# Sliding-window attention and a highway layer on one core: q and k loaded two tokens of each 64 to a partition, the set-up cut in pieces, the bias of 12 blocks added by ScalarE, and a new written order

## The chip, the core and the metric

The kernel runs on one core of a Trainium2 chip. The metric is the device time of one execution in microseconds (us). The engines are TensorE (PE; its weight loads are listed as PEld), VectorE (DVE), ScalarE (ACT), GpSimd (POOL) and SyncE (SP), each with a queue of its own that is worked off in order. An engine waits for another only where its next instruction needs it. Transfers are issued from POOL's queue (loads, with a cast from float32 to bfloat16) and SP's queue (stores), and run on 16 DMA engines.

## The reference

There are 8 batches, 8 heads, 576 tokens and a head size of 64. Attention is causal with a window of 128 tokens and a linear bias by distance (ALiBi); its output, heads side by side, is the input x of a highway layer.

```python
scores = scale * np.matmul(q, k.transpose(0, 1, 3, 2))
bias = slopes[:, None, None] * (-np.abs(rel))[None, :, :]
mask = (rel >= 0) & (rel < window)
scores = np.where(mask, scores + bias[None], -1000000000.0)
attn = softmax(scores)
x = np.matmul(attn, v)          # [4608, 512] after putting heads side by side
H = np.maximum(x @ w_h, 0.0)
T = 1.0 / (1.0 + np.exp(-(x @ w_t + b_t)))
return T * H + (1.0 - T) * x
```

q, k, v, the weights and the result are float32; the kernel multiplies in bfloat16.

## The kernel before

The work is cut into 32 stages of scores, four for each batch, and 36 blocks of 128 rows of x: four for each batch, and one for every two batches that holds the last 64 rows of both. All steps are small functions (`load`, `tr`, `scores` and so on). The string `ORDER` names one step per letter, and the letters are worked off from left to right; each engine's queue is the order in which its instructions come up. `BANKS` gives the PSUM bank of each step in turn.

A batch goes through these steps. POOL issues five loads (L111, L117): q and k for each group of four heads, and v. A q or k load puts 18 consecutive tokens of a head into each of 128 partitions, 4608 bytes read in one piece; v is read in pieces of 256 bytes. DVE transposes q and k in 32x32 squares of 4-byte words (`tr`, L178), so that a pair of head elements lies in a partition and the tokens lie along it; the words of a square's row are written 18 words, 72 bytes, apart. Two buffers of each hold the loads (`LD`) and the transposed data (`TR`), so every second batch uses the same one. PE makes the scores (`scores`, L206 and, in the last stage of a batch, L216), 32 small matmuls to a stage, each on 32 rows of the array. In eight stages, listed in `ADD`, PE first writes the bias and the mask into PSUM with four matmuls on a table `MA` (L198); POOL has made that table (L168). ACT takes the exponential (`soft`, L233). In the 24 other stages DVE multiplies the result by a table `MK` or `MK3` that holds the exponential of the bias, or zero outside the window (`mask`, L240).

PE multiplies by v in two halves (`pv`, steps p and y, L273); a column of ones beside v gives the sum for the softmax. Before each second half stands a drain of PE. DVE divides (`norm`, L282 and L283), PE transposes the block (L292), ACT copies it to SBUF (L297), and PE multiplies by `wH` (L302) and by `wT` (L323). The bias b_t is added to the second product by one more matmul with a row of ones (L325). What follows is elementwise: relu by ACT (L312, then a subtraction of x by DVE, L317) or by DVE alone (L308); tanh by ACT (L329); a scaling to the gate by ACT (L334) or DVE (L336); the product with the gate by DVE or POOL (L342); the final addition by POOL or DVE (L347); and the store from SP (L353, L357). Capital letters in `ORDER` choose the other engine.

The set-up stands at the head of `ORDER`: `clear` (step R) fills all constant parts of the buffers on DVE, then four loads are issued, then `setup` (step S) makes the tables on POOL, DVE and ACT. The first v load comes after it in POOL's queue. A load waits until the load eight before it has landed, since eight semaphores are used in turn.

Of the kernel before, what the change touches and what calls it, by code (L numbers as in the profile page):

```python
# [9 lines left out]
P = 128  # L10
NB, NS, NG, NH = 8, 4, 2, 4
NP, NP3, NT = 5, 3, 18
ADD = ((0, 1), (1, 1), (2, 1), (3, 1), (4, 1), (5, 1), (6, 1), (7, 1))

ORDER = (
    "RLLLLSTLTLLTLLTLLLsseesmLesepmpLyynnpxymcxchLnLpUhvxLTycznLhauTxtzUGcTzaLvthToazUgLdDOsa"
    "gdvesOLDdgsmeLToesLTdeppymyLnpnyxLTcxchnhTxzcuLUmsaheLvTpzUmLyasvnpTexyznLcTsaxheDDgLpTy"
    "cosuhGednzDOxLUmsdczavmephLDTaGyUsntGpTexyLzOcOdsanhLdeLvzguoxTascdpmehLDmyznUtppgaxvyOy"
    "cpndhnxUygzcnoxTaxhdcvcLDsmtLheuhgUpTGsUTLyepnyLnxscOzeOdxvdhvamcsDuhGeTpzoTUypLdanzLtvL"
    "smaxyemznGtsaTcGxtzTeopTyoadschnedhgDOUxuGsdcTpehOyvzdnUsmaxzemvptTypapycnytznxnaxhcgtTG"  # L20
    "xUscTGcheTohuhdUOsOUdzevdvvzmastmapzegmyoznatdDpmaxycppnypygxnyochnxdnhcuxUxgpcDhOvydGUh"
    "nzvuoxasdzctehGzUoascvdtmhageDpozUygdsanzeOxvdptsmaycgztnoehGdxuzaocpthmdayUDzGnpvaxgyoc"
    "pnhodyUxnzcdvDxahgcozuDdhgaOzUDdgvOaDdgOd"
)
BANKS = (
    "0404024010210402101240404602323014021402340124012430242014012402346020140124012402430140"
    "2146076045605460467045602540124012401420140260452320612134201402140124012302340201401201"
# [3 lines left out]
def lists():  # L31

    stages = [(b, s) for b in range(NB) for s in range(NS)]
    blocks = []
    for b, s in stages:
        blocks.append((b, s))
        if s == NS - 1 and b % 2:
            blocks.append((b // 2, NS))
    loads = []
    for b in range(NB):  # L40
        loads += [(w, b, g) for g in range(NG) for w in "kq"]
        loads += [("v", b)]
        if b == 0:
            loads += [("w", 0), ("w", 1), ("w", 2)]
    by = dict(L=loads, T=[x for x in loads if x[0] in "kq"])
    by.update({k: stages for k in "se"})
    by["m"] = [x for x in stages if x not in ADD]
    by["v"] = []
    by.update({k: blocks for k in "pynxchuzatgod"})
    return by  # L50
# [3 lines left out]
def kernel(  # L54
# [26 lines left out]
    SQ = S + 64  # L81
# [9 lines left out]
    LD = {(i, g, w): cp.tile([P, NT * D], BF16, name=f"ld{i}{g}{w}")  # L91
          for i in range(2) for g in range(NG) for w in "qk"}
    TR = {(i, g, w): cp.tile([P, SQ, 2], BF16, name=f"tr{i}{g}{w}")
          for i in range(2) for g in range(NG) for w in "qk"}
# [9 lines left out]
    MA = cp.tile([P, NH, 2, 192], BF16, name="ma")  # L104
    MK3 = cp.tile([P, NH, 2, 256], BF16, name="mk3")
    PS = pp.tile([P, 8, 512], F32, name="ps")

    def load(kind, *at):
        if kind in "qk":
            b, g = at  # L110
            nc.gpsimd.dma_start(  # L111
                out=LD[b % 2, g, kind][:],
                in_=(q if kind == "q" else k)[b, 4 * g : 4 * g + 4].rearrange(
                    "h (s t) d -> (h s) (t d)", t=NT))
# [13 lines left out]
    def clear():  # L128
        for i in range(NB):
            nc.vector.memset(VA[i][:, :, D : D + 1], 1.0)  # L130
        nc.vector.memset(ones0[:], 0.0)
        nc.vector.memset(ones0[0:1, :], 1.0)
        nc.vector.memset(ident[:], 1.0)
        for p in PB:
            nc.vector.memset(p[:, :, 0:64], 0.0)
            nc.vector.memset(p[:, :, 256:320], 0.0)
            nc.vector.memset(p[:, :, 512:576], 0.0)
        for p in PE3:
            nc.vector.memset(p[:, :, 0:64], 0.0)
        for i in range(2):  # L140
            for g in range(NG):
                for w in "qk":
                    nc.vector.memset(TR[i, g, w][:, S:SQ, :], 0.0)
        nc.vector.memset(bT[:], 0.0)

    def setup():
        rel_i = cp.tile([P, 192], I32, name="rel_i")
        rel = cp.tile([P, 192], F32, name="rel")
        over = cp.tile([P, 192], F32, name="over")
        for half in range(2):  # L150
            nc.gpsimd.iota(rel_i[half * D : (half + 1) * D, :], pattern=[[1, 192]], base=0,
                           channel_multiplier=-1)
        nc.gpsimd.affine_select(
            out=ident[:], in_=ident[:], compare_op=ALU.is_equal, fill=0.0,
            base=0, pattern=[[1, P]], channel_multiplier=-1)
        nc.vector.tensor_copy(out=rel[:], in_=rel_i[:])
        for op, edge in ((ALU.is_lt, 0.0), (ALU.is_ge, 128.0)):
            nc.vector.tensor_scalar(out=over[:], in0=rel[:], scalar1=edge, scalar2=65536.0,
                                    op0=op, op1=ALU.mult)
            nc.vector.tensor_tensor(out=rel[:], in0=rel[:], in1=over[:], op=ALU.add)  # L160
        for h in range(NH):
            for g in range(NG):
# [238 lines left out]
```

## Time and profile before

| what | value |
|---|---|
| median of three runs | 176.96 us (176.01 to 177.53) |
| profiled execution, its own time | 177.99 us |
| its span in the profile | 175.9 us |
| mean granted clock of PE | 0.973 |
| busy: PE, DVE, ACT, POOL | 137.9, 141.8, 112.6, 82.7 us |
| written by transfers from POOL's queue | 15.21 MB in 42688 packets |
| written by transfers from SP's queue | 9.44 MB in 5248 packets |

The profile is of one execution. Its own time is 2.1 us longer than its span, because the time also holds what lies before the first and after the last instruction of the profile. The busy time of PE is modelled and says when PE had matmuls in flight, not that it ran at its peak. The rows of groups give an instruction's line, engine, operation, shape and count, then its busy time and mean duration, then the idle time of the engine just before it and what ended it.

### The profile page before, as it was taken

Reading aid. Unit: us, or ns where it says so; the run is one execution under the profiler, and the core shown is the slowest. Engines: PE = TensorE matmul, PEld = TensorE weight load, DVE = VectorE, ACT = ScalarE, POOL = GpSimd, SP = SyncE. Lnnn points to the kernel's source line nnn. Section 1 sums busy time; section 2 is a strip of 40 time slices with the busy share of each in tenths; the row PEclk is TensorE's granted clock in tenths of the full one; section 3 lists DMA queues with packets and bytes.
Section 4 is the critical chain, followed back from the end, with each engine's and each line's share of the span. In section 5 each row is a group of like instructions: output and inputs, shape, how many; then the busy total and the mean of one; then the engine's idle time right before and its main releaser. Section 6 shows DMA issues by size and latency. Waiting matters only on the chain.

```text
span 175.9 us, 6252 instructions
## 1 busy us (share of the span) xinstructions
PE 137.9 (78%) x2711; PEld 75.4 (43%) x2740; DVE 141.8 (81%) x267; ACT 112.6 (64%) x155; POOL 82.7 (47%) x92
## 2 busy tenths in 40 slices
PE   0005599994899899799988886999999999999940
PEld 0002473543644454355544443555445554555410
DVE  6875375999878999789899697999979956769690
ACT  2223832789236787684876886987894559895540
POOL 7399454669134285520581965303431436178300
PEclk9999999999579999999999999999999999999997
DMA  3904999999999999999699899220131131322143
GB/s 62 196 12 32 170 206 211 167 202 266 206 209 168 199 175 241 202 227 231 174 133 174 224 159 206 79 60 4 62 120 63 63 119 63 101 82 112 72 159 82
DMA packets 47963, 25.04 MB, mean 142 GB/s; under 512 B 38208, under 2 KB 39232, under 8 KB 47936
## 3 DMA queue, kind: packets, MB, share of 16 engines
q0 software_dynamic: 42688, 15.21, 77.1%
q1 hardware_dynamic: 5248, 9.44, 15.7%
q8 instruction: 21, 0.34, 0.8%
q14 instruction: 6, 0.05, 0.1%
HBM read 30.41 MB, written 9.44 MB: 227 GB/s over the span
## 4 chain that ended last, share of the span: by engine, by line
PE 66%; DVE 11%; issue 8%; DMA 5%; ACT 4%; POOL 3%; DVEq 0%
PE ps L323 17%; PE ps L302 16%; PE ps L273 15%; PE ps L206 6%; PE ps L292 5%; DMA va<-in_v_dram 5%; PE ps L325 4%; POOL ma L168 3%; ACT p L233 2%; PE ps L198 2%; DVE ot L347 1%; DVE uu L342 1%; PE ps L216 1%; DVE x L283 1%; DVE uu L308 1%
## 5 line engine op out<-in xcount | busy, mean ns | idle before, releaser
L233 ACT ACTIVATE p<-ps 128x1536 bf16<-128x1536 f32 x24 | 34.6, 1455 | 12.2 <-PE ps L206 12.2
L302 PE MATMUL ps<-wH,xt 128*128 128x512 bf16 x127 | 36.1, 405 | 2.7 <-issue 1.6
L347 POOL TENSOR_TENSOR ot<-uu,x 128x512 f32<-128x512 bf16 x19 | 23.2, 1222 | 30.0 <-DVE uu L342 18.4
L323 PE MATMUL ps<-wT,xt 128*128 128x512 bf16 x133 | 35.9, 381 | 0.9 <-issue 0.5
L342 POOL TENSOR_TENSOR uu<-uu,tt 128x512 bf16<-128x512 bf16 x15 | 18.7, 1245 | 27.7 <-ACT tt L334 13.5
L329 ACT ACTIVATE tt<-ps 128x512 f16<-128x512 f32 x36 | 21.6, 600 | 14.4 <-PE ps L325 13.8
L273 PE MATMUL ps<-va,p 64*128 64x65 bf16 x768 | 25.4, 201 | 6.5 <-issue 1.7
L297 ACT COPY xt<-ps 128x512 bf16<-128x512 bf16 x36 | 20.8, 588 | 15.0 <-PE ps L292 14.7
L273 PEld LDWEIGHTS <-p 64*128 64x128 bf16 x768 | 18.4, 100 | 21.0 <-issue 19.2
L283 DVE TENSOR_TENSOR x<-ps,rd 128x512 bf16<-128x512 f32 x36 | 24.9, 691 | 1.3
L240 DVE TENSOR_TENSOR p<-p,mk 128x1536 bf16<-128x1536 bf16 x16 | 17.4, 1091 | 5.3 <-ACT p L233 5.3
L302 PEld LDWEIGHTS <-xt 128*128 128x128 bf16 x144 | 12.9, 102 | 14.6 <-issue 3.4
L312 ACT ACTIVATE uu<-ps 128x512 bf16<-128x512 f32 x24 | 14.3, 602 | 6.9 <-PE ps L302 6.1
L206 PE MATMUL ps<-tr00q,tr00k 32*64 32x192 bf16 x256 | 6.7, 281 | 14.4 <-DVE tr00q L178 13.4
L323 PEld LDWEIGHTS <-xt 128*128 128x128 bf16 x144 | 12.1, 98 | 12.2 <-issue 0.5
L117 POOL DMA_DIRECT2D va<-in_v_dram x8 | 14.8, 1852 | 4.8 <-DMA va<-in_v_dram 2.5
L233 ACT ACTIVATE r<-ps 128x2048 bf16<-128x2048 f32 x8 | 15.1, 1882 | 2.7 <-PE ps L216 2.7
L317 DVE TENSOR_TENSOR uu<-uu,x 128x512 bf16<-128x512 bf16 x24 | 11.3, 483 | 6.4 <-ACT uu L312 6.4
L282 DVE RECIPROCAL rd<-ps 128x8 f32<-128x8 f32 x36 | 7.1, 198 | 10.2 <-PE ps L273 9.9
L292 PE MATMUL ps<-ident,x 128*128 128x128 bf16 x144 | 14.3, 230 | 0.4 <-DVE x L283 0.4
L325 PE MATMUL ps<-bT,ones 128*128 128x512 bf16 x35 | 13.3, 380 | 0.5 <-issue 0.5
L292 PEld LDWEIGHTS <-x 128*128 128x128 bf16 x144 | 10.2, 103 | 6.1 <-issue 0.9
(77 smaller groups left out, 205.2 us busy)
## 6 DMA issues: line engine op xcount, KB each, us to landing
out_dram<-ot SPq DMA_DIRECT2D x32, 256.0 KB, 3.0
va<-in_v_dram POOLq DMA_DIRECT2D x8, 576.0 KB, 14.1
ld00k<-in_k_dram POOLq DMA_DIRECT2D x4, 288.0 KB, 12.7
ld00q<-in_q_dram POOLq DMA_DIRECT2D x4, 288.0 KB, 12.8
ld01k<-in_k_dram POOLq DMA_DIRECT2D x4, 288.0 KB, 11.5
ld01q<-in_q_dram POOLq DMA_DIRECT2D x4, 288.0 KB, 10.7
ld10k<-in_k_dram POOLq DMA_DIRECT2D x4, 288.0 KB, 13.2
ld10q<-in_q_dram POOLq DMA_DIRECT2D x4, 288.0 KB, 13.4
```

Of the source, the lines that this page charges most:

```text
L233: nc.scalar.activation(out=pview(b, s), in_=SC.pop((b, s))[:, :, 0:n].rearrange("p h (g n) -> p h g n", g=NG), func=ACTF.Exp, scale=scale)
L240: nc.vector.tensor_tensor(out=p, in0=p, in1=(MK3 if s == 3 else MK)[:], op=ALU.mult)
L273: mm = nc.tensor.matmul(out=av[o : o + m, par, j * (D + 1) : (j + 1) * (D + 1)], lhsT=PT[bb, st][rows, h, c : c + m], rhs=VA[bb][rows, at ...
L283: nc.vector.tensor_tensor(out=x[:].rearrange("p (i r d) -> p r i d", i=NH, r=2), in0=av[:, :, :, 0:D], in1=rd[:].to_broadcast([P, 2, NH, D ...
L292: nc.tensor.transpose(out=pt[:, c * P : (c + 1) * P], in_=X[b, s][:, c * P : (c + 1) * P], identity=ident[:])
L297: nc.scalar.copy(out=xt[:].rearrange("p c n -> p (c n)"), in_=XP.pop((b, s)))
L302: nc.tensor.matmul(out=pa, lhsT=XT[b, s][:, c, :], rhs=wH[:, c, :], start=c == 0, stop=c == NC - 1)
L323: nc.tensor.matmul(out=pz, lhsT=xt[:, c, :], rhs=wT[:, c, :], start=c == 0, stop=False)
L325: nc.tensor.matmul(out=pz, lhsT=ones0[:], rhs=bT[:], start=False, stop=True)
L329: nc.scalar.activation(out=tt[:], in_=PZ.pop((b, s)), func=ACTF.Tanh, scale=0.5)
L342: eng.tensor_tensor(out=uu, in0=uu, in1=TT.pop((b, s))[:], op=ALU.mult)
L347: eng.tensor_tensor(out=ot[:], in0=UU.pop((b, s))[:], in1=X[b, s][:], op=ALU.add)
```

## The change

q and k are loaded in four loads each to a batch, one for every two heads, to 32 partitions. A partition holds two consecutive tokens of every 64, in pieces of 512 bytes read and 256 written. One transpose now covers all heads of q or of k in a batch, 1152 words to a partition, and the words of a row are written two words, 8 bytes, apart. The two heads that share rows of the array lie one behind the other in `TR`, so head numbers and the halves of the score tiles change in `scores` and `pv`, and the buffers of the last stage (`PE3`) are 640 wide in place of 576.

`ADD` is empty: DVE multiplies by the mask in all 32 stages, and `MA` is not made. In 12 of the 36 blocks a step b lets ACT copy the bias from a float32 tile `bA`, which SP loads at the start to all partitions, into the PSUM bank; the four matmuls with `wT` then add to it, and the matmul with ones is left out. `clear` and `setup` are cut in pieces that the order places one by one, ACT fills both mask tables, and four of the 36 drains are left out. `ORDER` now gives each step with its number, and is new throughout, `BANKS` too. The engines of the elementwise steps are: gate product 28 on DVE and 8 on POOL (before 21 and 15), final addition 12 on DVE and 24 on POOL (before 17 and 19), scaling 24 on DVE and 12 on ACT (before 18 and 18).

The new order begins with these steps, a letter and a number each (Q, R, P, A are pieces of `clear`; B, S, r, k pieces of `setup`; L loads q or k, V loads v, W a weight):

```text
Q00 L00 B00 R00 L01 L02 P00 L03 L04 L05 L06 S00 L07 r00 W00 V00 T00 k00 L08 W01 T01 L09 W02 s00 L10 s01 e00
```

The core of the diff:

```diff
-ADD = ((0, 1), (1, 1), (2, 1), (3, 1), (4, 1), (5, 1), (6, 1), (7, 1))
+ADD = ()
+BIAS = True
...
-        loads += [(w, b, g) for g in range(NG) for w in "kq"]
+        loads += [(w, b, h) for w in "kq" for h in (0, 2, 1, 3)]
...
-    PE3 = [cp.tile([P, NH, 576], BF16, name=f"r{i}") for i in range(NP3)]
+    PE3 = [cp.tile([P, NH, 640], BF16, name=f"r{i}") for i in range(NP3)]
...
-                out=LD[b % 2, g, kind][:],
-                in_=(q if kind == "q" else k)[b, 4 * g : 4 * g + 4].rearrange(
-                    "h (s t) d -> (h s) (t d)", t=NT))
+                out=LD[b % 2, kind][32 * h : 32 * h + 32],
+                in_=(q if kind == "q" else k)[b, NG * h : NG * h + NG].rearrange(
+                    "g (n s t) d -> s (g n) (t d)", s=32, t=2))
...
+        elif step == "k":
+            for tab in (MK, MK3):
+                for h in range(NH):
+                    for g in range(NG):
+                        nc.scalar.activation(out=tab[:, h, g, 0:192], in_=rel[:], func=ACTF.Exp,
+                                             scale=-slopes[NG * h + g])
+            for half in range(2):
+                rows = slice(half * D, (half + 1) * D)
+                nc.scalar.copy(out=MK3[rows, :, half, 192:256], in_=MK[rows, :, half, 0:D])
+        else:
+            nc.sync.dma_start(
+                out=bA[:], in_=moe_b_t.rearrange("(o n) -> o n", o=1).broadcast_to([P, DM]))
...
-            out=TR[b % 2, g, w][:, 0:S].rearrange("p s e -> p (s e)").bitcast(U32).rearrange(
-                "p (s t) -> p t s", t=NT),
-            in_=LD[b % 2, g, w][:].bitcast(U32).rearrange("p (t i) -> p t i", i=32))
+            out=TR[b % 2, w][:, 0 : NG * S].rearrange("p s e -> p (s e)").bitcast(U32).rearrange(
+                "p (n s t) -> p n t s", s=32, t=2),
+            in_=LD[b % 2, w][:].rearrange("p n x -> p (n x)").bitcast(U32).rearrange(
+                "p (n t i) -> p n t i", t=2, i=32))
...
-                        rows, half, t = slice(32 * h, 32 * h + 32), (h + i) % 2, 2 * s + i
+                        rows, half, t = slice(32 * h, 32 * h + 32), (g + i) % 2, 2 * s + i
...
-        else:
+        elif fence:
             nc.tensor.drain()
...
+    def bias(b, s):
+        pz = PZ[b, s] = take(1)[:, 0, :]
+        nc.scalar.copy(out=pz, in_=bA[:])
+
     def mm_z(b, s):
...
             nc.tensor.matmul(out=pz, lhsT=xt[:, c, :], rhs=wT[:, c, :],
-                             start=c == 0, stop=False)
-        nc.tensor.matmul(out=pz, lhsT=ones0[:], rhs=bT[:], start=False, stop=True)
+                             start=c == 0 and not given, stop=c == NC - 1 and given,
+                             skip_group_check=given)
+        if not given:
+            nc.tensor.matmul(out=pz, lhsT=ones0[:], rhs=bT[:], start=False, stop=True)
```

More of the change, by code (lines that the diff above doesn't have):

```diff
@@ L44, in lists @@
             loads += [("w", 0), ("w", 1), ("w", 2)]
[L45 to L49, printed above, removed]
+    by = dict(V=[x for x in loads if x[0] == "v"], W=[x for x in loads if x[0] == "w"])
+    by["L"] = [x for x in loads if x[0] in "kq"]
+    by["T"] = [(w, b) for b in range(NB) for w in "kq"]
+    by.update({k: stages for k in "sem"})
+    by.update({k: blocks for k in "pynxchuvbzatgod"})
     return by
@@ L126, in load @@
                 out=bT[0:1, :], in_=moe_b_t.rearrange("(o n) -> o n", o=1))
[L128 to L162, printed above, removed]
-                nc.scalar.activation(out=MK[:, h, g, :], in_=rel[:], func=ACTF.Exp,
-                                     scale=-slopes[4 * g + h])
-        nc.vector.memset(MK3[:], 0.0)
+    def pads(i):
+        for w in "qk":
+            nc.vector.memset(TR[i, w][:, NG * S :, :], 0.0)
@@ L166, in setup, with additive @@
+    def additive():
         for h in range(NH):
@@ L201, in scores @@
         for g in range(NG):
+            g0 = g * S
             for e in range(2):
@@ L312, in relu_sub @@
             nc.scalar.activation(out=uu[:], in_=PA.pop((b, s)), func=ACTF.Relu)
-            by["v"].append((b, s))
     def sub_x(b, s):
```

157 lines of the change are left out of this document (107 added, 50 removed).

## The prediction

> **What bounds the kernel now.** First the engine table and the slices, to see which engine is full and when; of the slices, PE's row is the one to read.
>
> ```profile
> span 175.9 us, 6252 instructions
> PE 137.9 (78%) x2711; PEld 75.4 (43%) x2740; DVE 141.8 (81%) x267; ACT 112.6 (64%) x155; POOL 82.7 (47%) x92
> ...
> PE   0005599994899899799988886999999999999940
> DVE  6875375999878999789899697999979956769690
> ```
>
> A slice is 4.4 us. PE does nearly nothing in the first five slices, is then almost full to the end, and DVE is almost as full. Second the chain of work that ended last, by engine: mostly PE, with DVE as the runner-up.
>
> ```profile
> PE 66%; DVE 11%; issue 8%; DMA 5%; ACT 4%; POOL 3%; DVEq 0%
> ```
>
> Third the same chain in order of time and the timeline of the first 30 us, to see what PE's late start waits for.
>
> ```profile
> 8.37 2.91 POOL ma L168 x4
> ...
> 13.62 8.28 DMA va<-in_v_dram
> 22.03 0.84 PE ps L273 x24
> ...
> 85.11 1.16 DVE tr01q L178
> ...
> 89.14 1.17 DVE tr10k L178
> 90.31 1.08 DVE tr10q L178
> ```
>
> POOL makes the additive bias table (L168) before it issues the first v load, so v lands at 21.9 and the first P·V product (L273) starts at 22.03. From there the chain is PE for most of the time; between 84.4 and 92.2 us it is DVE, three of whose transposes (L178) are on it. Fourth, busy time by stretch:
>
> ```profile
> 40.00:50.00 10.00, 6.91 (x157) 4.46 (x143) 9.00 (x14) 5.05 (x5) 4.68 (x5) 0.68 1.60 234
> ...
> 110.00:130.00 20.00, 19.19 (x391) 10.41 (x391) 19.57 (x33) 17.25 (x24) 4.96 (x4) 1.00 0.21 71
> ```
>
> The columns after the length are busy us of PE, PEld, DVE, ACT and POOL, then the granted clock, the DMA share and GB/s. From 110 to 130 PE and DVE are both full: work taken off one alone would leave the other. At 40 to 50 the granted clock is 0.68: PE waited 3 to 4 us for three exponentials of ACT (38.1 to 42.2), and the clock is 0.50 from about 43.6 to 50.4, which costs half of 6.8 us.
>
> **Part 1, transposes (DVE).** The rows of the groups, line, engine, operation, shapes, count, busy us, mean ns:
>
> ```profile
> L178 DVE STREAM_TRANSPOSE tr10k<-ld10k 128x576 uint32<-128x576 uint32 x4 | 5.0, 1250 | 0.0
> L283 DVE TENSOR_TENSOR x<-ps,rd 128x512 bf16<-128x512 f32 x36 | 24.9, 691 | 1.3
> L160 DVE TENSOR_TENSOR rel<-rel,over 128x192 f32<-128x192 f32 x2 | 0.7, 359 | 0.1
> L130 DVE MEMSET va<- 128x36 bf16 x8 | 0.7, 88 | 1.5 <-PEq L385 1.0
> ```
>
> 32 transposes of 576 words at 1.24 us are 39.8 us. Each writes words 72 bytes apart. The change makes 16 of 1152 words, written 8 bytes apart. An operation on 4-byte elements costs (691 - 359)/(512 - 192) = 1.04 ns an element over a fixed 0.16 us, so 576 words ought to take 0.76 us, and the row is 1.24. If the stride is what costs the difference, 1152 words take 1.36 us; 16 are 21.8 us, a saving of 18.0. At the old rate (about 1.9 ns a word, from the 1.08 us between starts of back-to-back transposes) one takes 2.3 us and the saving is 3. No row shows a transpose at another stride. I take 1.36, as one element per 1.04 ns is what the other 4-byte rows do, and keep 2.3 for the range.
>
> [...] A row speaks against it: the memset above writes 36 elements 130 bytes apart in 88 ns and shows no such penalty; if that row decided for transposes too, the old rate would stay, which is the last rival below.
>
> **Part 2, eight masks back on DVE, eight additions off PE.** PE loses 32 matmuls of 384 columns (L198). Four take 0.65 to 0.76 us from their start to the next one's; seven of the eight groups lie behind the first P·V: 7 x 0.70 = 4.9 us off a full engine. DVE gains 8 multiplications at 1.09 us (L240), 8.7 us. POOL loses the 5.95 us of L168 ahead of the v load.
>
> **Part 3, bias by ScalarE in 12 of 36 blocks.** PE loses 12 matmuls of 512 columns (L325), each 0.22 to 0.31 us from its start to the next: 3.0 us. ACT gains 12 copies of 128x512 into PSUM. No row writes PSUM from ACT; the nearest are L297 (588 ns) and L312 (602 ns), the bounds by length 0.59 and 0.66 us. I take 0.60: 7.2 us. The copies stand one or two steps ahead of their products, behind exponentials of up to 1.88 us; what waits for a late copy is PE's queue.
>
> **Part 4, set-up and shifts between engines.** ACT fills the second mask table itself: 8 exponentials at 0.27 (eight took 2.13) and two copies, 3 us; DVE loses 2.0 us there. Gates move POOL to DVE (21 to 28, at 0.49 against 1.25), final additions the other way (17 to 12, at 0.68 against 1.22), six scalings of ACT go to DVE (0.64 against 0.34). Four of 36 PE drains go, about 0.1 us each. Sums: DVE 141.8 - 18.0 + 8.7 - 2.0 + 2.0 + 3.4 - 3.4 = 132.5; PE 137.9 less about 8 of the time its queue needs; ACT 112.6 + 7.2 + 3 - 3.8 = 119.
>
> **Part 5, the loads.** 32 loads of 128 packets become 64 of 576 packets (two tokens, 256 bytes written), and go to 32 partitions each. Issue on POOL:
>
> ```profile
> L117 POOL DMA_DIRECT2D va<-in_v_dram x8 | 14.8, 1852 | 4.8 <-DMA va<-in_v_dram 2.5 <-DMA ld10q<-in_q_dram 2.1 <-issue 0.2
> L121 POOL DMA_DIRECT2D wH<-in_moe_w_h_dram x1 | 0.8, 769 | 0.0
> L111 POOL DMA_DIRECT2D ld01q<-in_q_dram x4 | 2.2, 548 | 2.5 <-DVE uu L317 1.6 <-DMA ld10k<-in_k_dram 0.5 <-issue 0.4
> ```
>
> 128 packets cost 0.55 us, 512 cost 0.77, 4608 cost 1.85: bounds 0.68 (a line through the outer two) and 0.79. I take 0.75, nearest the weights: 64 x 0.75 = 48 us against 17.9. POOL becomes 82.7 + 30.1 - 5.7 - 8.7 + 6.1 = 104.5 us. POOL is idle over half the span now, and the loads end at two thirds of the order; but among the loads in POOL's queue stand gates and final additions (8 and 24 in all), on which SP's stores wait, and each load waits until the load eight before it has landed, which used to be 1.6 batches back (five loads a batch) and is now 0.9 (nine).
>
> Transfer: in the DMA view of the first stretches 4608-byte reads run at about 200 GB/s written (1.47 us a load, 184 ns a packet on each of 16 engines) and v's 256-byte reads at 157 (3.76 us, 13 ns). A straight line between these gives 23 ns for a 512-byte read, 0.83 us a load; bounds 0.74 (equal bytes per us) and 0.94 (v's rate). A batch of q, k and v takes 8 x 0.83 + 3.76 = 10.4 us against 9.6, while PE needs some 16 for a batch: hidden. If loads ran at half the rate it would not be (second rival).
>
> **The start.** POOL now issues seven loads, iota and select (1.0 us), the eighth, wH and then v: v is issued by 11.2 us. The transfers run from 2.7 us: bA 1.3 (256 KB from SP, the same engines), 8 x 0.83, wH 2.6, v 3.76, and about 1 us to landing, as v's first load shows: 18.0 us. The other way to the first P·V: last q load landed 11.8, transposed 13.1, scores 13.7, ACT free of its tables at 14.2 (5.1 us from 9.1), exponential 15.7, mask 16.8. So v still ends last, 4.0 us earlier than 22.0.
>
> **The sum.** From the profiled span of 175.9: start 4.0, additions 4.9, bias 3.0, drains 0.4. Of the stall at 38 to 50 I take 2 us of waiting and half of the clock's 3.4, since the new order puts products between the exponentials there; of the DVE stretch at 80 to 100 (PE idle 2.9 us), 2.0. That is 18.0. Against it I charge 3 us for tighter queues: ACT goes from 0.72 to about 0.81 of the time behind the start, POOL from 0.5 to 0.7. An estimate from these shares, and it can be 0 or 9. Net 15: span 160.9. The profiled run's own time was 177.99, 2.1 above its span and 1.0 above the median of the three runs (176.96): 177.99 - 15 = 163.0 in its terms, 162.0 in the median's.
>
> **Rivals.** (1) The order wins nothing: PE's waits grow by what its work shrinks, only part of the start is kept: about 175. For it: from 110 to 130 three engines are at 0.96, 0.98 and 0.86, so queues in a written order can easily wait for one another. Against it: both of the full ones get shorter.
>
> (2) The loads bind. If a load to 32 partitions runs at half of 200 GB/s, 1.47 us, then eight take 11.8 us, the first v lands 5 us later, and a batch takes 15.5 us, which together with stores is PE's pace: 162 + 5 + 3 = 170. For it: the DMA row of the page stands at 9 from slice 4 to 22 already. Against it: v's packets of half the size reach 157. [...] No run here has shown a 32-partition load.
>
> (3) Slower: the transposes keep their rate, and DVE decides. DVE's sum is then 132.5 + 15 = 147.5, 5.7 above now. With DVE at 0.98 in its full stretches there is no cover, and PE's savings turn into waiting: 176.96 - 4.0 (start) + 8.7 (masks that no transposes pay for) = 181.7. It decides from the point where a transpose of 1152 words costs over 2 us; below 1.6 it is dead. For it: the memset row. Against it: 1.24 us has no other explanation in the rows.
>
> **How the numbers follow.** Forecast 162 (own range 154 to 168): 0.65. Loads bind, 170: 0.15. Order wins nothing, 175 to 178: 0.06. DVE decides, 181.7: 0.14. One per cent is 1.8 us, about what a measurement of this kernel can tell from no change. Faster by more than that holds the first two, 0.80; within it 0.06; slower 0.14. The range 154 to 174 holds the first two, 0.80.
>
> **What would show it.** Right: transposes (L211) near 1.36 us; first P·V at 18 us; 64 loads near 0.75 us of issue and landing without holding PE; POOL near 104 us, DVE near 132; twelve copies near 0.60. Wrong: transposes above 2 us; q or k loads landing more than 6 us after issue in the first 12 us; PE waiting for tr, or DVE for loads, after 40 us; POOL's gates and additions waiting behind loads and holding the x or u buffers; a granted clock at 0.5 more than once.

## The result and the profile after

The changed kernel takes 183.37 us in the median of four runs (181.75 to 185.44); the kernel before took 177.25 beside it (176.01 to 177.75). The ratio is 1.033, with a 95% interval of 1.023 to 1.042: slower, where 162 was forecast. Comparisons leave disturbed runs out; where too few were left, an experiment below has a median and no interval, and its lowest run is the one to compare. Ratios are always to the kernel before on the same chip.

The page of the profile after, engine table and slices (a slice is 4.5 us):

```profile
span 181.8 us, 6238 instructions
PE 136.0 (75%) x2696; PEld 75.2 (41%) x2696; DVE 142.4 (78%) x263; ACT 117.8 (65%) x171; POOL 102.2 (56%) x114
...
PE   0006499946799989639998859989797799979850
...
DVE  7644495475569999825999999889999978999990
...
PEclk9999999995869999956999996999999799999998
DMA  5999999999994999999679999996741320133352
```

PE's row now has holes: the 4 at 36 to 41 us and the 6 and 3 at 73 to 82 us. Each has a dip of the granted clock beside it (the row PEclk). The mean granted clock is 0.93 where it was 0.973: half clock for 6.8 us from 40.3, 3.4 from 50.6, 6.8 from 77.9, 3.4 from 108.6 and 3.4 from 142.7, 23.9 us in all, against a single stretch of 6.8 us before. The chain by engine, and parts of it in order of time (start, length, what):

```profile
PE 30%; DVE 26%; DMA 15%; issue 10%; ACT 8%; POOL 8%; DVEq 0%; POOLq 0%; ACTq 0%
```

```profile
8.72 11.49 DMA va<-in_v_dram
20.34 0.84 PE ps L306 x24
...
62.60 13.60 DMA va<-in_v_dram
76.24 0.29 PE ps L306 x8
76.54 3.50 issue
80.04 0.40 PE ps L306 x8
```

PE has fallen from 66% of the chain to 30%; DMA has risen from 5 to 15. Two v loads take 11.5 and 13.6 us from issue to landing. The first sets the first P·V at 20.34. For the second PE waited only 0.32 us, so its length in the chain is not a cost; behind it PE stands still for 3.50 us with nothing named as the cause ("issue"). Long times to landing alone do not show late loads: their medians were 14.1 us for v and 10.7 to 13.4 for q and k in the kernel before, and are 12.9 and 5.1 to 11.8 now. Busy time by stretch, columns as before, of the changed kernel:

```profile
40.00:50.00 10.00, 6.03 (x126) 3.85 (x127) 5.96 (x10) 3.56 (x6) 4.44 (x6) 0.66 2.73 136
110.00:130.00 20.00, 17.81 (x404) 9.87 (x397) 18.04 (x28) 16.82 (x20) 7.20 (x8) 0.95 1.53 154
20.00:110.00 90.00, 73.80 (x1465) 40.69 (x1465) 69.46 (x115) 57.42 (x79) 65.36 (x72) 0.90 2.06 157
```

and of the kernel before over the stretch in which loads run:

```profile
20.00:110.00 90.00, 77.33 (x1593) 42.56 (x1607) 76.63 (x122) 61.06 (x78) 44.94 (x47) 0.96 1.49 199
```

From 20 to 110 us PE makes 1465 matmuls where it made 1593, POOL is busy 65 us in place of 45, and the transfers move 157 GB/s in place of 199, while the share of the DMA engines (the time that packets took over the time of 16 engines) goes up from 1.49 to 2.06. The groups that the prediction priced:

```profile
L211 DVE STREAM_TRANSPOSE tr0k<-ld0k 128x1152 uint32<-128x1152 uint32 x4 | 5.5, 1372 | 0.0
L353 ACT COPY ps<-bA 128x512 f32<-128x512 f32 x12 | 7.1, 592 | 1.8 <-DVE uu L341 1.7
L128 POOL DMA_DIRECT2D ld1q<-in_q_dram x16 | 10.8, 676 | 6.8 <-DMA va<-in_v_dram 4.5 <-DMA wT<-in_moe_w_t_dram 1.2 <-DMA wH<-in_moe_w_h_dram 0.9
L273 DVE TENSOR_TENSOR p<-p,mk 128x1536 bf16<-128x1536 bf16 x24 | 29.0, 1209 | 7.7 <-ACT p L266 7.7
```

Transposes, copies and issues cost what was forecast. The masks cost more (1209 ns against 1091). POOL's loads wait 10.1 us in all for others to land, no more than the 11.5 of the kernel before.

### The profile page after: what moved, and what is told of

Its sections match the earlier page's. It is cut to its first block, busy times and chain, and to the rows that moved or that the text cites. A ratio compares the mean times of both kernels' runs of the same rounds, so it can differ in the third digit from the quotient of the medians.

```text
span 181.8 us, 6238 instructions
## 1 busy us (share of the span) xinstructions
PE 136.0 (75%) x2696; PEld 75.2 (41%) x2696; DVE 142.4 (78%) x263; ACT 117.8 (65%) x171; POOL 102.2 (56%) x114
## 3 DMA queue, kind: packets, MB, share of 16 engines
q1 hardware_dynamic: 5392, 9.70, 16.4%
## 4 chain that ended last, share of the span: by engine, by line
PE 30%; DVE 26%; DMA 15%; issue 10%; ACT 8%; POOL 8%; DVEq 0%; POOLq 0%; ACTq 0%
DMA va<-in_v_dram 14%; PE ps L306 9%; PE ps L335 8%; DVE p L273 6%; PE ps L362 6%; PE ps L325 4%; ACT p L266 4%; DVE uu L383 4%; DVE r L273 3%; POOL ld0k L128 3%; POOL ld0q L128 3%; ACT uu L345 2%; DVE tt L377 2%; DVE x L316 2%; DVE uu L349 2%
## 5 line engine op out<-in xcount | busy, mean ns | idle before, releaser
L388 POOL TENSOR_TENSOR ot<-uu,x 128x512 f32<-128x512 bf16 x24 | 31.7, 1331 | 40.0 <-DVE uu L383 20.3
L335 PE MATMUL ps<-wH,xt 128*128 128x512 bf16 x144 | 38.9, 405 | 0.0
L362 PE MATMUL ps<-wT,xt 128*128 128x512 bf16 x144 | 38.4, 397 | 0.6 <-DVE x L316 0.6
L273 DVE TENSOR_TENSOR p<-p,mk 128x1536 bf16<-128x1536 bf16 x24 | 29.0, 1209 | 7.7 <-ACT p L266 7.7
L383 POOL TENSOR_TENSOR uu<-uu,tt 128x512 bf16<-128x512 bf16 x8 | 10.8, 1351 | 18.9 <-DVE tt L377 10.5
L241 PE MATMUL ps<-tr0q,tr0k 32*64 32x192 bf16 x512 | 9.8, 276 | 14.7 <-DVE tr0q L211 13.2
L362 PEld LDWEIGHTS <-xt 128*128 128x128 bf16 x144 | 13.5, 101 | 15.0 <-issue 2.9
L335 PEld LDWEIGHTS <-xt 128*128 128x128 bf16 x144 | 13.3, 104 | 14.6 <-issue 3.9
L325 PE MATMUL ps<-ident,x 128*128 128x128 bf16 x144 | 16.1, 250 | 0.3 <-DVE x L316 0.3
L383 DVE TENSOR_TENSOR uu<-uu,tt 128x512 bf16<-128x512 bf16 x28 | 15.0, 549 | 0.4 <-ACT tt L375 0.2
L134 POOL DMA_DIRECT2D va<-in_v_dram x8 | 14.6, 1831 | 0.0
L128 POOL DMA_DIRECT2D ld1q<-in_q_dram x16 | 10.8, 676 | 6.8 <-DMA va<-in_v_dram 4.5
## 6 DMA issues: line engine op xcount, KB each, us to landing
va<-in_v_dram POOLq DMA_DIRECT2D x8, 576.0 KB, 12.9
ld1k<-in_k_dram POOLq DMA_DIRECT2D x16, 144.0 KB, 11.8
```

The costliest lines, as they stand in the source:

```text
L128: nc.gpsimd.dma_start(out=LD[b % 2, kind][32 * h : 32 * h + 32], in_=(q if kind == "q" else k)[b, NG * h : NG * h + NG].rearrange("g (n s ...
L273: nc.vector.tensor_tensor(out=p, in0=p, in1=(MK3 if s == 3 else MK)[:], op=ALU.mult)
L325: nc.tensor.transpose(out=pt[:, c * P : (c + 1) * P], in_=X[b, s][:, c * P : (c + 1) * P], identity=ident[:])
L335: nc.tensor.matmul(out=pa, lhsT=XT[b, s][:, c, :], rhs=wH[:, c, :], start=c == 0, stop=c == NC - 1)
L362: nc.tensor.matmul(out=pz, lhsT=xt[:, c, :], rhs=wT[:, c, :], start=c == 0 and not given, stop=c == NC - 1 and given, skip_group_check=given)
L383: eng.tensor_tensor(out=uu, in0=uu, in1=TT.pop((b, s))[:], op=ALU.mult)
```

## The experiments

Three theories: the loads of the new layout hold the kernel (packets, POOL's issue of them, waits for their landing); the new order makes engines wait for one another; and, formed after the first runs, PE runs out of instructions, since a block of them comes late by DMA (the page counts 21 packets, 0.34 MB, on a queue "instruction").

### Layout and order apart, with and without loads

Four kernels change one side alone. `e1_wide` reads q and k in pieces of 4608 bytes (tokens then lie in another order in the tiles):

```diff
-  out=LD[b % 2, kind][32*h : 32*h+32],
-  in_=...rearrange("g (n s t) d -> s (g n) (t d)", s=32, t=2)
+  out=LD[b % 2, kind][32*h : 32*h+32].rearrange("p n x -> p (n x)").rearrange("p (g y) -> p g y", g=NG),
+  in_=...rearrange("g (s t) d -> s g (t d)", s=32)
```

> The changed kernel, with each q or k load read in 64 pieces of 4608 bytes in place of 576 of 512; the same bytes go to the same tiles, so a tile holds tokens in another order and the scores are not the reference's; all else is as in the changed kernel. Loads theory (the small packets keep the 16 DMA engines and POOL's queue busy so long that v, and PE's instruction fetches, come late; PE stalls and its clock is halved): about 166 us (162 to 171), no PE gap over 2 us behind the first P-V product, half clock for under 10 us in place of 24. Order theory (the written order itself costs the time, whatever the loads take): 179 to 184 us, the gaps stay.

Measured: 178.48 us, ratio 1.007 (1.003 to 1.012), outside both expectations. By the ratios the big packets give back 4.5 us of the loss, 1.6 of them at the start (first P·V at 18.71). PE's gaps stay, the longest 4.32 us and again "issue", with 17 us of half clock.

`e2_half` keeps the 576 packets and halves their bytes from batch 2 on:

```diff
+  m = 2 if b < 2 else 1
-  out=LD[b % 2, kind][32*h : 32*h+32],
+  out=LD[b % 2, kind][32*h : 32*h+32, :, 0 : m*D],
```

> The changed kernel, with the q and k loads of batches 2 to 7 still in 576 packets, but of half the bytes (256 read, 128 written; the other half of each tile keeps what an earlier batch left there, which is left out of the loads). POOL's issue time stays at 0.67 us a load. If the time in the DMA engines is what hurts: a load takes about 0.47 us in place of 0.83, some 17 us of transfer less over the kernel, and about 172 us (167 to 176). If POOL's issue time is what hurts, or the number of packets ahead of an instruction fetch: 179 us or more. Order theory: 179 to 184.

Measured: 181.63 us, 1.027 (1.018 to 1.036). By the ratios half the bytes of q and k give back 1.0 us, which is within the intervals, and the longest gap of PE is again 4.32 us. So the time of these packets in the DMA engines is not the price.

`e3_old_layout` has the order, masks and bias of the change with the loads and transposes of before:

```diff
-  LD, TR: two tiles for q, two for k; 8 loads of 576 packets, 2 transposes a batch
+  LD, TR: four tiles each; 4 loads of 128 packets, 4 transposes a batch
```

> The changed kernel's order, masks and bias, with the loads, transposes and tiles of the kernel before (four loads of 128 packets to a batch for q and k, words written 72 bytes apart). Loads theory: the v loads come in time, but DVE gains 32 transposes at 1.24 us for 16 at 1.38, 17.6 us, and is the bound: 180 to 186 us, with DVE busy about 158. Order theory: slower than the changed kernel by most of the 17.6 us, 192 to 200.

Measured: 184.25 us, 1.042 (1.033 to 1.050), in the range of the loads theory, with DVE busy 154.3 us. But gaps of 2.73 and 2.54 us ended by "issue" stay, so the small packets are not needed for them, and without its new layout the change loses as much.

`e4_layout_only` has the order, additions and bias of before with the new loads and transposes:

```diff
-ADD = ()
-BIAS = True
+ADD = ((0, 1), (1, 1), (2, 1), (3, 1), (4, 1), (5, 1), (6, 1), (7, 1))
+BIAS = False
+ORDER, BANKS: those of before, each L of a group replaced by two loads
```

> The kernel before with its own order, its additions on PE and no bias copies, and only q and k loaded and transposed the new way (each old load becomes two new ones at its place, each first pair of transposes of a batch becomes the two new ones). Loads theory: DVE is 18 us shorter, but the packets and POOL's issue time are as in the changed kernel: 176 to 184 us, v loads landing late and half clock periods again. Order theory: the shorter transposes show, 166 to 172 us.

Measured: 189.59 us, 1.074 (1.067 to 1.080), above both expectations, with DVE busy 127.0 us where it was 141.8. Work of 15 us less on DVE went with a kernel 13 us longer.

The next four take the q, k and v loads of batches 2 to 7 out; all work on PE, DVE and ACT stays.

```diff
 def load(kind, *at):
+    if kind in "qkv" and at[0] >= 2:
+        return
 ...
-    rhs=VA[bb][rows, at // 2, :]
+    rhs=VA[bb % 2][rows, at // 2, :]
```

In the changed kernel:

> The changed kernel without the q, k and v loads of batches 2 to 7: the transposes of those batches read again what batches 0 and 1 left, and their P*V products read v of batch 0 or 1. All work on PE, DVE and ACT stays, in the same order. POOL loses 48 q/k loads at 0.68 us and 6 v loads at 1.85 us. Loads theory (packets, their issue on POOL and the waits for their landing hold the new order): about 168 us, PE's gaps above 1 us after the first 30 us gone. Order theory (in the written order the engines wait for one another whatever the loads do): 178 to 183 us, gaps of 2 to 4 us near 40 and near 77 us still there. Instruction theory (PE runs dry when its next 16 KB of instructions come late): the gaps near 40 and 77 us go if the loads' packets are what makes the fetch late, with about 168 us; they stay if the fetch is late by itself, then 178 to 183 us.

Measured: 168.31 us, 0.950 (0.933 to 0.967). Its engine table, and the stretch from 20 to 110 us:

```profile
PE 129.9 (78%) x2666; PEld 74.2 (45%) x2696; DVE 137.7 (83%) x263; ACT 117.3 (70%) x171; POOL 60.3 (36%) x60
```

```profile
20.00:110.00 90.00, 81.89 (x1730) 46.72 (x1744) 78.17 (x136) 69.76 (x94) 30.30 (x25) 0.94 0.39 73
```

1730 matmuls in the stretch that held 1465. The holes near 40 and 77 us are gone. The first stretch of half clock is not: it lasts 6.8 us from 39.4 us here. Both kernels work off the same DVE queue, so the starts of its reciprocals (one to a block) show where the time is lost:

```text
block                       0     3     4     8    12    14    18    22    25    35
changed kernel           21.7  29.6  42.9  53.8  74.7  84.9 103.1 120.3 131.7 168.8
without those loads      21.1  28.9  39.1  48.5  68.4  73.1  90.5 105.6 116.3 153.7
behind by                 0.6   0.8   3.8   5.2   6.3  11.8  12.6  14.7  15.3  15.1
```

Three steps, before block 4, at blocks 7 and 8, and at blocks 13 and 14, make 9.9 of the 15 us; each lies at a hole of PE ended by "issue" (39.77, 48.81 and 76.54 us), with half clock behind it. After block 25, when the loads have ended, nothing more is lost.

In the kernel before:

> The kernel before without the q, k and v loads of batches 2 to 7, in the same manner. Loads theory and instruction theory: the old order had few waits for loads and short PE gaps, so 173 to 177 us; what the pair of runs without loads then shows is the worth of the new order and layout by themselves: 168 against 175. Order theory: 175 to 177 us, with the changed kernel without loads above it.

Measured: 171.49 us, 0.971 (0.962 to 0.979), below what any theory had. With the old layout in the new order:

> The changed kernel's order, masks and bias with the old loads and transposes (184.25 us), without the q, k and v loads of batches 2 to 7. If the new order pays for loads whatever their packets: 168 to 172 us, 12 to 16 us below, like the pair with the new layout. If it is the new layout's packets and their issue that cost there, and here the slow transposes: 176 to 179 us, 5 to 8 us below, like the kernel before.

Measured: 175.67 us, 0.994 (0.990 to 0.998), next to the second range. With the new layout in the old order:

> The old order, additions and bias with the new layout (189.6 us), without the q, k and v loads of batches 2 to 7. If the loads of the new layout are all that costs there: 164 to 169 us, below the old layout without loads (171.5), as DVE has 18 us less to do. If the old order cannot use faster transposes, or the layout costs something besides loads: 171 to 176 us.

Measured: 174.27 us, 0.974 (0.966 to 0.981), in the second range. The eight together, ratios turned into us at 177.25 for the kernel before:

```text
                           with loads   without   loads cost
old order, old layout        1.000       0.971       5.2 us
old order, new layout        1.074       0.974      17.7 us
new order, old layout        1.042       0.994       8.4 us
new order, new layout        1.033       0.950      14.6 us
```

The last column is uncertain by 2 to 3 us. The loads of the old layout cost 5 to 8 us in either order, those of the new one 15 to 18. Without loads the new layout is worth 7.8 us in the new order and nothing in the old one, where DVE has time left. Without loads the new order with its masks and bias costs 4 us with the old layout and wins 4 with the new one, so its masks need the fast transposes. In the new order the new loads cost 6.2 us more than the old ones, and 1.6 of the 7.8 is left, less than the intervals can tell; in the old order they cost 12.5 more. The change as a whole saves 3.7 us without these loads, and its loads cost 9.4 more than those before.

### What of the loads it is

`e9_no_v` leaves out the v loads alone, `e10_no_qk` those of q and k alone, again from batch 2 on, by the same early return.

> The changed kernel without the v loads of batches 2 to 7 alone (their P*V products read v of batch 0 or 1); all q and k loads stay. The changed kernel without any of these loads took 168.3 us, with all 183.4. If the waits for v's landings (14 per cent of the chain) are the price: 170 to 172 us. If the small packets of q and k and POOL's time to issue them are: 178 to 181 us.

Measured: 173.78 us (169.26 to 175.09; no interval). By its lowest run, leaving v out gives back 14 us.

> The changed kernel without the q and k loads of batches 2 to 7 alone (their transposes read again what batches 0 and 1 left); all v loads stay. If the small packets of q and k and POOL's time to issue them are the price: 169 to 172 us. If v's loads are: 178 to 181 us.

Measured: 171.55 us, 0.969 (0.961 to 0.977). Both expectations were of one guilty part, and neither kind is it alone: q and k left out give back 11.4 of the 14.6 us, v up to 14. It is the two kinds together that cost. `e12_sp_traffic` moves these loads to SP's queue and into scratch tiles:

```diff
+  if kind in "qk" and at[0] >= 2:
+      nc.sync.dma_start(out=SCR[kind == "q"][32*h : 32*h+32], in_=<the same pieces>)
+      return
+  if kind == "v" and at[0] >= 2:
+      nc.sync.dma_start(out=SCV[:], in_=<the same pieces>)
+      return
```

> The changed kernel with its q, k and v loads of batches 2 to 7 put on SP's queue, in the same pieces and at the same places of the order, into scratch tiles that nobody reads: the reads from memory and their number stay (written as f32, twice the bytes in SBUF), POOL issues none of them, no transpose and no product waits for one. If the traffic as such makes PE's instructions come late: 176 to 181 us, with PE gaps of 2 us and more behind a packet of the instruction queue again. If POOL's issue and the waits for landings are the price: 168 to 171 us, no such gaps. SP's own stores may come late behind them; that would show at the end of the span and not in PE's gaps.

Measured: 196.97 us, 1.105 (1.091 to 1.119), outside both expectations. The first P·V starts at 44.31, behind a wait of 11.45 us for v's landing; that it landed late because SP, which has nobody to wait for in these loads, issued them at once is the author's reading. From that start to the end of the span (193.0) it takes 148.7 us, against 161.5 in the changed kernel (181.8 - 20.34) and 146.9 without the loads (166.6 - 19.77). The granted clock is 0.98. Part of this traffic ran ahead of the first P·V, but from 70 to 126 us transfers still moved 238 GB/s beside the work. So here packets in such numbers cost little (148.7 against 146.9 us), with nobody waiting for them and POOL not issuing them. Whether it is POOL's time to issue, the landings, or the kind of transfer that POOL's queue makes (the page counts it as software_dynamic, SP's as hardware_dynamic), this run does not tell.

### PE's instructions

The page of the changed kernel counts 21 packets on the queue "instruction", 0.34 MB, 16 KB each. The trace has one from 39.5 to 41.0 and one from 77.3 to 78.5 us, and PE starts again at 42.46 and 80.04, 1.4 and 1.6 us behind their ends. At the start of the first of the two, PE had begun 959 instructions in the changed kernel; without the loads the corresponding packet came at 811, and PE did not stop. PE's three holes by "issue" begin behind 961, 1217 and 2241 of its instructions (drains counted), 256 and 1024 apart; its 5434 instructions are 259 to each of the 21 packets. That a packet brings a block of some 256 instructions is an estimate from these counts, and `e7_shift` is to move the borders of such blocks:

```diff
-T00
+X64 T00    # 64 matmuls of 128x64 on ones0, before PE has other work
```

> The changed kernel with 64 extra products of 128x64 at the start, ahead of the first transpose, when PE has nothing to do. They add 128 instructions to PE's stream (half of a 16 KB block), so every later block boundary comes 128 instructions earlier. Instruction theory: PE's gaps near 40, 49 and 77 us move to other instructions, 128 PE instructions earlier or vanish, each still ending some 1.5 us after a packet of the instruction queue; the time moves by several us either way. Order and loads theories: the gaps stay ahead of the same steps of the order, and the time is within 1 per cent of 183.4.

Measured: 183.79 us, 1.039 (1.023 to 1.054). The hole at 76.5 of the changed kernel (first row, its timeline of PE, with the idle time ahead in brackets) became two in the shifted one (the other rows):

```profile
80.04 0.40 PE L306 MATMUL ps<-va,p 64*128 64x65 bf16 x8 [3.50 <-issue]
```

```profile
75.38 0.21 PE L307 MATMUL ps<-va,p 64*128 64x65 bf16 x2 [1.88 <-issue]
...
83.18 0.25 PE L307 MATMUL ps<-va,p 64*128 64x65 bf16 x5 [2.16 <-issue]
```

They end 1.4 and 1.5 us behind packets of that queue that end at 74.0 and at 81.7. The hole at 39.8 is gone; one of 2.03 us from 45.2 on, which the profile puts down to ACT, ends 1.8 us behind a packet (45.4). The holes follow the packets and not the steps, as the instruction theory said; that the time would move by several us did not come. Next, PE's longest waits behind the first P·V (us in all, times, longest): first in the changed kernel, then in the same without the loads of batches 2 to 7, last PE's only one for DVE in the kernel before.

```profile
PE ps L306 <- issue: 8.1, 7, 3.5
PE ps L306 <- DVE x L316: 4.2, 4, 2.0
PE ps L306 <- DVE p L273: 3.0, 2, 2.0
```

```profile
PE ps L308 <- DVE x L318: 3.5, 4, 2.0
PE ps L308 <- DVE p L275: 2.4, 3, 1.1
...
PE ps L308 <- issue: 0.8, 5, 0.2
```

```profile
PE ps L292 <- DVE x L283: 0.4, 1, 0.4
```

The waits for DVE stay without the loads, those by "issue" nearly go. Idle times of PE over 0.5 us ended by "issue" sum to 7.5 us in the changed kernel, 4.6 in the kernel before, and 0.0 in all six kernels without the loads of batches 2 to 7. With SP's traffic 2.2 are left: one hole of 1.44 us ends 1.6 us behind a packet (92.84), and PE had begun 2224 matmuls and weight loads there, as many as at the hole of 3.50 us above. So these holes come with loads, and more of them with POOL's (7.5 us) than with SP's (2.2). Whether a late packet causes them, and why it comes late beside loads, is not shown.

### The parts off PE

`e8_masks_only` is the kernel before with the additions replaced by masks on DVE:

```diff
-ADD = ((0, 1), (1, 1), (2, 1), (3, 1), (4, 1), (5, 1), (6, 1), (7, 1))
+ADD = ()
-"...sseesmL..."
+"...sseemsmL..."    # an m right behind the e of each such stage; MA is not made
```

> The kernel before with one part of the change alone: the masks of stage 1 of each batch are multiplied on DVE right behind their exponentials, the 32 additions on PE and the additive table on POOL are gone. By the prediction's terms: start 4.0 us earlier, PE's queue 4.9 us shorter, DVE 8.7 us longer. PE decides: 169 to 172 us. DVE decides (order theory: work moved on to DVE comes back as waiting of PE): 180 to 183 us.

Measured: 174.02 us, 0.984 (0.973 to 0.995), between the two.

```profile
PE 130.2 (76%) x2679; PEld 71.9 (42%) x2708; DVE 148.8 (86%) x275; ACT 112.8 (65%) x155; POOL 79.7 (46%) x84
```

DVE at 148.8 us is over the 147.5 at which the third rival had it decide, and the kernel got faster: DVE's sum as such is no bound. But 1.5 us come from the start (first P·V at 20.49 against 22.03), and only about 2 us of the 4.9 off PE arrive behind it. The same without loads:

> The kernel before with the masks of stage 1 on DVE and without the q, k and v loads of batches 2 to 7 (171.5 us with the additions; their ratio with all loads was 174.0 to 178.7). If the additions off PE are worth their 4.9 us behind the first P*V: 165 to 167 us. If DVE's 8.7 us more take that back and only the start stays: 168 to 171 us.

Measured: 174.71 us (171.79 to 175.12; no interval). The lowest run is level with the 171.49 of the kernel that has the additions, and none is near 165 to 167: no gain shows. Whether DVE's 8.7 us take it back is not shown.

`e13_no_copies` and `e14_few_loads_no_copies` give the bias back to PE, with all loads and without those of batches 2 to 7:

```diff
 def bias(b, s):
     pz = PZ[b, s] = take(1)[:, 0, :]
-    nc.scalar.copy(out=pz, in_=bA[:])
 def mm_z(b, s):
-    given = (b, s) in PZ
+    given = False
```

> The changed kernel with the 12 bias copies of ScalarE taken out and the bias of these blocks added again by a fifth product on PE; the banks are taken at the same places of the order. ACT loses 7.1 us, PE gets 3.0 us back. If PE's length is what counts (the prediction's step): 185 to 187 us. If the copies hold PE or ACT's other work more than they save: 177 to 182 us. No difference beyond 1 per cent: the part is worth nothing either way.

> The same edit in the changed kernel without the q, k and v loads of batches 2 to 7 (168.3 us with the copies). If PE's length counts once the loads are gone: 170 to 172 us. If the copies eat their saving: 164 to 168 us.

Measured: 183.73 us, 1.037 (1.030 to 1.044), and 168.33, 0.948 (0.942 to 0.955), next to 183.37 and 168.31 with the copies. 3.0 us off PE and 7.1 on ACT: worth nothing that these intervals, of about 1 per cent, can tell either way.

`e11_masks_bias` puts the 12 copies into the old order, with the masks:

```diff
-"...vthToaz..."
+"...vthbToaz..."    # b up to three steps ahead of its z, 12 times
```

> The kernel before, its order and its loads, with the masks of stage 1 on DVE (as in the run with this part alone, 174.0 us) and the bias of the change's 12 blocks copied by ScalarE, the copy up to three steps ahead of its products. Next to the run with the changed kernel's order and the old loads (184.25 us) it differs in little but the order. If the new order is what costs there: 171 to 174 us. If bias copies cost (PE waits for ACT at each): 177 us or more.

Measured: 181.44 us, 1.011 (0.996 to 1.026). Its output is not the reference's, for a cause not found; the work is the same. It was meant to leave only the order between itself and `e3_old_layout`, but the copies cost here: 0.984 without them. Placed like this they do harm, so the pair does not tell the order's share.

### A version ahead of both

`e17_masks_early_start` is `e8_masks_only` with the set-up in pieces: first what batch 0 and the distances need, then the four transposes, then the second mask table and the other constants.

```diff
-"RLLLLSTLTLLTLLTLLLsseemsmL..."
+"RLLLLSTLTLLTTKLLLLLsseemsmAL..."    # K: MK3, PE3, bT; A: PB 3 and 4, TR 1, VA 1 to 7
```

> The kernel before with the masks of stage 1 on DVE and a set-up in pieces: ahead of the first transposes DVE only clears what batch 0 needs and makes the table's distances; the second mask table and the rest of the clearing follow the four transposes. All of the computation is there. With the masks alone the first transpose started at 11.1 us behind the mask table and the first P*V at 20.5, while v landed at 15.9. If the start is set by DVE's set-up: first P*V at 16.5 to 17.5 us, 170 to 171 us. If the loads' landing sets it: first P*V at 19 to 20, 172.5 to 174 us. If what is won at the start is lost again at the stall of three exponentials near 36 to 42 us (loads theory: the later loads are no earlier): 173 to 174 us with an early first P*V.

Measured: 175.29 us beside 178.82 for the kernel before, 0.976 (0.968 to 0.984).

```profile
span 171.1 us, 6212 instructions
PE 134.9 (79%) x2708; PEld 72.4 (42%) x2708; DVE 149.9 (88%) x275; ACT 112.8 (66%) x155; POOL 79.8 (47%) x84
```

The first P·V starts at 16.46 us, where DVE's set-up was to put it, 4.0 us earlier than with the masks alone, but the span is only 1.3 us shorter (171.1 against 172.4). The ratio is 0.007 better, and the intervals overlap: what is won at the start is mostly lost again, as the third expectation had it. At block 0 the kernel is 4.1 us ahead of the one before (first reciprocal 19.3 against 23.4), at block 4 3.5 (40.8 against 44.3), with a hole of 1.78 us in PE ended by "issue" ahead of it and the same 6.8 us of half clock. It is ahead of both kernels, of the one before by 2.4 per cent.

## Why the prediction was wrong

Predicted span 160.9, measured 181.8: 20.9 us, of which 2.3 lie ahead of the first P·V (20.34 for 18.0) and 18.6 behind it (161.5 for 142.9).

What was right: the transposes (1.36 forecast; 1.37 in three groups, 1.41 in the fourth), the copies (0.60; 0.592), the issue of a load (0.75; 0.67 to 0.68), POOL (104.5; 102.2), ACT (119; 117.8). The trace agrees with the element rate of 1.04 ns: 1.37 us for the one transpose 8 bytes apart, where two 72 bytes apart took 2.48. What makes those slower is not shown. The last rival is dead by its own bound of 1.6 us: that the kernel got slower, as it alone had forecast (181.7), is luck. Of the signs of being wrong, q or k landing more than 6 us after issue (10.6 for one issued at 10.5 us) and a clock at 0.5 more than once did come.

The start. v was issued at 8.7 us, 2.5 earlier than forecast, and landed 2 later. The term that was mis-sized is the transfer of v, 3.76 us as if nothing came behind it in the queues: `wT` and the loads of batch 1 were issued ahead of it or while it ran. Its packets start at 13.2 us, as in the sum, and end at 18.9, 5.7 us later.

The loads, "hidden". This step failed, and it is the largest: 14.6 us measured between the kernels with and without the loads of batches 2 to 7, where about 1 was left in the sum. (Before, the loads cost 6.7 behind the first P·V, 153.9 against 147.2 in spans; the prediction's 3.7 and 2.0 of stalls to be won were most of that.) The step set a batch's transfers, 10.4 us, against PE's 16 and took the smaller for hidden. It left the stores out, which the page's table of queues counts on the same 16 engines: 16.4% of the span on SP's queue is 29.8 us, 3.7 a batch, and makes it 14.1, an estimate and still below 16. The rate of a load was right, in the middle of the kernel too. Transfers of the changed kernel from 74 to 76 us and from 40 to 42 us:

```profile
DMA packets 1453, 0.36 MB, mean 178 GB/s; under 512 B 1452, under 2 KB 1452, under 8 KB 1453
```

```profile
DMA packets 2019, 0.26 MB, mean 131 GB/s; under 512 B 2019, under 2 KB 2019, under 8 KB 2019
```

The first are packets of 248 bytes on average, nearly all of q and k, at the 0.83 us a load of the prediction; the second, of 129 bytes, are v's, which fell below their 157. So the step did not fail by the price of a load, and half the bytes changed little. What it had no term for is PE's idle time ended by "issue". In waits of 0.2 us and more PE stands 9.0 us by "issue" with the loads and 1.6 without them, 7.4 of the 14.6; and half clock lasts 23.9 us with them and 13.6 without, which costs 5.1 at most, an estimate at the half that the prediction took. The rest is not traced. The kernel before stands 7.1 us by "issue", and 2.1 without the loads: its loads were not hidden either. The second rival named the loads, but by a load at 1.47 us, half of the 200 GB/s of the old loads. No run shows such a load: to 32 partitions they ran at the 178 GB/s above, 0.83 us each. That its 170 lies nearer is luck.

The work off PE. The terms 4.9, 3.0 and 0.4 less 3 for tighter queues should have left 5.3 us behind the first P·V. Without loads the two orders need 146.9 and 147.2: 0.3 was left. Here the first rival was right in kind: PE's waits grew by what its work shrank. Behind the first P·V PE waits 7.4 us for DVE in the changed kernel without loads and 0.8 in the kernel before without them. The copies show no gain in two pairs of runs, and the masks give back most of theirs.

DVE, 132.5 forecast, 142.4 measured. The means of the rows were taken as prices, and the means rose: masks by 118 and 172 ns (32 of them, 4.2 us), gates from 490 to 549 (1.7), scalings from 339 to 448 (2.6); 8.5 of the 9.9 us. Without the later loads DVE is busy 137.7 us, so 4.7 of the 9.9 come with the loads and 5.2 with the order.

The stall at 38 to 50 was to shrink by half. PE still waits 0.80 and 0.56 us for the exponentials (before: 0.34, 0.79 and 0.56, 1.7 us in all where the prediction read 3 to 4), an idle time of 2.68 us ended by "issue" comes on top, the 6.8 us of half clock stay, and a second stretch of 3.4 follows. The first stretch is not that idle time's doing: it stands without the loads too, where no idle time of PE over 0.80 us lies in the 13 us ahead of it.

## What to carry to other kernels

That a round of all transfers takes less time than the fullest engine needs does not show that the loads are hidden: here it was 14.1 us against 16, and the loads cost 14.6 us over the kernel, about half of it in waits of PE that no load's price holds. Run the kernels before and after without their later loads early on: such pairs split 21 us of error into loads and the rest. Work taken off the fullest engine was worth nothing here where it went to engines that it waits for in a written order.

## What the chip showed that was not expected

- PE stands still for 1.3 to 4.3 us with nothing named as the cause ("issue"), and starts again 1.4 to 1.6 us behind the end of a 16 KB packet on the queue "instruction" (1.41, 1.42 and 1.55 in the changed kernel). This happened beside loads issued by POOL, in every kernel with the new order and all loads (up to 2.4 us in the old order). That PE has run out of instructions there is the author's reading and not shown.
- Half clock lasts 3.4 or 6.8 us at a time in the changed kernel and 6.8 in the kernel before. No long idle time was needed ahead of it: without the later loads the clock falls at 39.4 us, with no idle time of PE over 0.80 us ahead of it, though PE was busy only 0.82 of the 2 us from 36 to 38.
- A mask of 1536 elements takes 0.95 us, and 1.90 (at 98.15 and at 101.24 us) where POOL is issuing a v load, or 2.10 (at 105.66) beside an addition on POOL and the issue of a k load. Not every mask beside them is stretched: 0.95 at 70.20 beside the issue of a v load, and at 113.70 beside an addition. Without the later loads four masks still take 1.90, beside additions and a gate product. Beside the issue of q or k loads alone (at 58.56 and 61.55) it keeps 0.91 and 0.94. The transposes were not stretched: their means are 1.37 to 1.41.
